# Chunked attention and two mixtures of experts: outputs of two attention tiles and scores of the next two in one run of small products

## Chip, cores and metric

The kernel runs on one core of a Trainium2 chip. The metric is the device time of one execution in microseconds (us). The core has TensorE (PE: matrix products; its weight loads are listed apart as PEld), VectorE (DVE), ScalarE (ACT), GpSimd (POOL) and SyncE (SP, which issues DMAs). Products are written to PSUM, which has eight banks of 512 fp32 columns on each of the 128 partitions.

## Reference

```python
def _attn_ref(q, k, v):                     # B, H, S, D = 8, 8, 576, 64
    q_c = q.reshape(B, H, nc, 64, D)        # chunks of 64 positions; k_c, v_c alike
    scores = scale * np.matmul(q_c, k_c.transpose(0, 1, 2, 4, 3))
    scores = scores - np.max(scores, axis=-1, keepdims=True)
    attn = np.exp(scores)
    attn = attn / (np.sum(attn, axis=-1, keepdims=True) + 1e-09)
    return np.matmul(attn, v_c).reshape(B, H, S, D)

def _moe_ref(x, w1, w2, w3, w_out):         # x 4608 x 512, w 512 x 768
    h = np.maximum(np.maximum(x @ w1, x @ w2), x @ w3)
    return h @ w_out

def _moe2_ref(x, w_gate, w_output_gate, w1, w2):   # 8 experts, 512 -> 1024 -> 512
    e_idx = np.argmax(x @ w_gate, axis=1)
    ...                                     # gate_w: softmax at e_idx; eom: sigmoid
    for e in range(E):
        mask = e_idx == e
        out[mask] = gate_w * eom[mask, e] * (np.maximum(x[mask] @ w1[e], 0.0) @ w2[e])
```

## The kernel before

The program has two parts, one after the other, and TensorE works through both.

**First part: attention and the first mixture.** The 4608 tokens are 36 tiles of 128, in nine blocks of four. A tile has two chunks of 64 positions and eight heads, so its scores are 16 products of 64x64 (line 440, `att_S`), and its outputs 16 more (line 520, `att_V`; line 518 for the first four tiles). Between the two lie the softmax (DVE maximum, ACT exponentials, DVE or POOL division) and four transposes of the probabilities into the PSUM bank `tr0` or `tr1` by the tile's parity (`att_P`, line 495), which ACT copies to `pTF` (line 501). Outputs go to SBUF in two parts, high (`xth`, ACT, line 532) and low (`xtl`, DVE). Scores and outputs share the two banks of one PSUM tile `a2`: scores in one half of each bank, outputs in the other (`quarters`). From tile 7 on `att_V(i)` issues the outputs of tile i and the scores of tile i+1 as one piece. The mixture's products (`moe_f`, 18 groups of 12 products of 128x512 for a block; `moe_y`, products of 256 or 272 columns) fill TensorE's time between; three products (lines 102 to 104) make one of higher precision.

The order of the first part isn't written by hand. Every operation is recorded with `add(...)`: engine, a duration, a due time (`prio`), and the keys that it reads and writes. `order()` then plays the program through with these durations and issues, on each engine, the ready operation with the earliest due time; the result is a fixed order for each engine. Waits between engines are set afterwards by the tile framework, from the tiles that the instructions read and write. In the first 30 us the planner also puts in small bf16 products that compute nothing (`warm`, line 291), written to whichever of `tr1`, `psg`, `tr0` is free.

**Second part: the routed experts.** 21 blocks of up to 256 tokens are run, each with its expert's weights (`step(b)`, and block 0 by lines of its own behind line 1247). A block with two tiles of tokens ("full") takes the first branch of `step`: the first layer (`l1_mm`), the transposes of the next block's tokens (`x_T`), the second layer of tile 0 (`l2(b, 0)`: 24 products of 128x512 into `ps_y[0]`), `y_act(b, 0)` (line 930: ACT reads `ps_y[0]`, scales it and writes `yo`), and `l2(b, 1)` into `ps_y[1]`. `ps_y` is another name for the two banks `tr0` and `tr1`. Other blocks take the second branch, with `l2(b, 0)` alone.

```python
    ps_y = ps_tr
...
            convs(b, 1)
            l2(b, 0)
            y_act(b, 0)
            l2(b, 1)
```

Of the kernel before, what the change touches and what calls it, by code (L numbers as in the profile page):

```python
# [10 lines left out]
F32 = mybir.dt.float32  # L11
# [10 lines left out]
def tile_chunk_attention_moe_moe(  # L22
# [16 lines left out]
    PE, ACT, DVE, POOL, SP = nc.tensor, nc.scalar, nc.vector, nc.gpsimd, nc.sync  # L39
# [7 lines left out]
    P = 128  # L47
    NTILE = NT // P
# [16 lines left out]
    tile_block = {}  # L65
# [10 lines left out]
    psp = ctx.enter_context(tc.tile_pool(name="psp", bufs=1, space=bass.MemoryType.PSUM))  # L76
# [16 lines left out]
    NAT, SUBD = 4, (0, 2)  # L93

    def f(ap):
        return ap.bitcast(F32)

    def sub(eng, o, a, b):
        eng.tensor_tensor(out=o, in0=a, in1=b, op=ALU.subtract)  # L99
# [72 lines left out]
    HP = H // 2  # L172
# [6 lines left out]
    v_buf = [part(n, i, 1).rearrange("p (h c d) -> p h c d", h=HP, c=2) for n, i in ((1, 2), (1, 3), (2, 3))]  # L179
    es = [part(2, i, 1).rearrange("p (h j) -> p h j", h=H) for i in range(3)]  # L180
    pTF = [part(3, i, 1).rearrange("p (a c i) -> p a c i", a=HP, c=2) for i in range(2)]
# [56 lines left out]
    rfv = gview(2 * TB, F32, "p (a t) -> p a t", t=TB)  # L238


    ps_tr = [psp.tile([P, 512], F32, name=f"tr{i}", tag=f"tr{i}") for i in range(2)]
    ps_a2 = psp.tile([P, 1024], F32, name="a2", tag="a2")
    ps_mm = [psp.tile([P, 512], F32, name=f"mm{i}", tag=f"mm{i}") for i in range(3)]
    ps_g = psp.tile([P, 512], F32, name="psg", tag="psg")
# [114 lines left out]
    def t_act(n):  # L359
        return 0.055 + n / 1200  # L360

    def t_dve(n, fast=False):
        return 0.067 + n / (1920 if fast else 960)
# [34 lines left out]
    def h64(h2):  # L398
        return slice(64 * h2, 64 * h2 + 64)
# [3 lines left out]
        i = a % NE2  # L403
        return es[i], [("e", i), ("mx", i), ("sm", i)], mxs[i], sms[i]

    def quarters(a, h=0):


        sp = lambda x, n: x.rearrange("p (b x) -> p b x", b=n)[:, :, h * HP * 64:(h + 1) * HP * 64].rearrange(
            "p b (a i) -> p b a i", a=HP)  # L410
        if a % 3 and a < NW:
            bk = [(ps_mm[0], ("mm", 0)), (ps_mm[1], ("mm", 1))] if a % 3 == 1 else [(ps_mm[2], ("mm", 2)), (ps_g, "psg")]
            return [(sp(x, 1), [kx], slice(i, i + 1)) for i, (x, kx) in enumerate(bk)]
        return [(sp(ps_a2, 2), ["a2"], slice(0, 2))]

    def add_sub(eng, n, prio, rd, wr, o, a, b):
# [5 lines left out]
    def att_Q(a, pr):  # L422
        for w in range(2):
            load(a, w, pr - LA)

    def att_S(a, pr, alone=True):


        e, (ek, mk, sk), mx, sm = e_of(a)

        t = qk_buf[a % 3]
        parts = quarters(a)
        bank = [ps[:, i] for ps, _, hs in parts for i in range(hs.stop - hs.start)]

        def mm():
            for hp in range(HP):
                for h2 in range(2):
                    for c in range(2):
                        x = t[h64(h2), :, hp, h64(c)]
                        PE.matmul(bank[h2 if a < NAT else h2 ^ c][h64(c), hp], x[:, 0], x[:, 1], start=True, stop=True)  # L440

        if not alone:
            yield mm
        else:
            add("PE", T_Q, pr + 1, [("qk", a % 3, 0), ("qk", a % 3, 1)], [x for _, kk, _ in parts for x in kk], mm)
        m2 = mx.rearrange("p (b a) -> p b a", b=2)
        for n, (ps, pk, hs) in enumerate(parts):
            add("DVE", t_dve(512 // len(parts)), pr + 1, pk, [(mk, n)],
                lambda ps=ps, hs=hs: DVE.tensor_reduce(out=m2[:, hs], in_=ps, axis=AX.X, op=ALU.max))
        ex = e.rearrange("p (a b) j -> p b a j", b=2)  # L450
        ek2, sk2 = [(ek, 0), (ek, 1)], [(sk, 0), (sk, 1)]
        if a in SUBD:
            for n, (ps, pk, hs) in enumerate(parts):
                add("DVE", t_dve(512 // len(parts)), pr + 1, pk + [(mk, n)], ek2 if len(parts) == 1 else [(ek, n)],
                    lambda ps=ps, hs=hs: DVE.tensor_tensor(
                        out=ex[:, hs], in0=ps, in1=m2[:, hs].unsqueeze(3).to_broadcast([P, hs.stop - hs.start, HP, 64]),
                        op=ALU.subtract))
            add("ACT", t_act(512), pr + 1, ek2, ek2, lambda: ACT.activation(out=e, in_=e, func=ACTF.Exp, scale=scale))
            add("DVE", t_dve(512), pr + 1, ek2, sk2, lambda: DVE.tensor_reduce(out=sm, in_=e, axis=AX.X, op=ALU.add))
        else:  # L460
            add("DVE", 0.08, pr + 1, [(mk, n) for n in range(len(parts))], [mk] + [(mk, n) for n in range(len(parts))],
                lambda: DVE.tensor_scalar(out=mx, in0=mx, scalar1=-scale, scalar2=None, op0=ALU.mult))  # L462
            for b in range(2):
                ps, pk, hs = parts[b % len(parts)]

                def fn(b=b):
                    for hp in range(HP):
                        ACT.activation(  # L468
                            out=ex[:, b, hp], in_=bank[b][:, hp], func=ACTF.Exp, scale=scale,
                            bias=mx[:, HP * b + hp:HP * b + hp + 1], accum_out=sm[:, 2 * hp + b:2 * hp + b + 1])  # L470

                add("ACT", 4 * 0.29, pr + 1, pk + [mk], [(ek, b), (sk, b)], fn)
        add("DVE", 0.08, pr + 1, sk2, sk2,
            lambda: DVE.tensor_scalar(out=sm, in0=sm, scalar1=1e-9, scalar2=None, op0=ALU.add))
        add("DVE", 0.12, pr + 1, sk2, sk2, lambda: DVE.reciprocal(out=sm, in_=sm))
        on = "DVE" if a < MULD else "POOL"
        add(on, t_dve(512) if on == "DVE" else 1.0, pr + 1, ek2 + sk2, ek2,
            lambda: (DVE if on == "DVE" else POOL).tensor_tensor(
                out=e, in0=e, in1=sm.unsqueeze(2).to_broadcast([P, H, 64]), op=ALU.mult))
        yield  # L480
# [19 lines left out]
        add("PE", 0.9 if a < NAT else 0.45, pr + 2, [(ek, 0), (ek, 1)], [("tr", a % 2)], fn)  # L500
        add("ACT", t_act(512), pr + 2, [("tr", a % 2)], [("pTF", a % 2)], lambda: ACT.copy(pTF[a % 2], pp))

    def att_V(a, pr, score=None):

        j, t_ = tile_block[a]
        dst = lambda hl: xt[j % 2][hl][:, :, t_ * P:(t_ + 1) * P]
        xk = lambda hl: [("xt", j % 2, t_, hl, h2) for h2 in range(2)]
        vv, x = v_buf[a % NV], pTF[a % 2]
        parts = quarters(a, 1 if score else 0)
        bank = [ps[:, i] for ps, _, cs in parts for i in range(cs.stop - cs.start)]  # L510
        with_it = next(score) if score else None

        def mm():
            for hp in range(HP):
                for s in range(2):
                    for c in range(2):
                        if a < NAT:
                            PE.matmul(bank[c][h64(s), hp], vv[h64(c), hp, s], x[h64(c), hp, s], start=True, stop=True)
                        else:
                            PE.matmul(bank[c][h64(s ^ c), hp], vv[h64(s), hp, c], x[h64(s), hp, c], start=True, stop=True)  # L520

            if with_it:
                with_it()

        qk = [("qk", (a + 1) % 3, w) for w in range(2)] if score else []
        add("PE", 2 * T_Q - 0.3 if score else T_Q, pr + 3, [("v", a % NV), ("pTF", a % 2)] + qk,
            [x for _, kk, _ in parts for x in kk], mm)
        o = lambda hl: dst(hl).rearrange("p a (b i) -> p b a i", b=2)
        for ps, pk, cs in parts:
            n = 256 * (cs.stop - cs.start)  # L530
            kx = lambda hl: [("xt", j % 2, t_, hl, i) for i in range(cs.start, 2)] if n == 256 else xk(hl)
            add("ACT", t_act(n), pr + 3, pk, kx(0), lambda ps=ps, cs=cs: ACT.copy(o(0)[:, cs], ps))
            add("DVE", t_dve(n), pr + 3, pk + kx(0), kx(1), lambda ps=ps, cs=cs: sub(DVE, o(1)[:, cs], ps, f(o(0)[:, cs])))


    def words(src):
# [559 lines left out]
    def attention(a, n):  # L1096

        def prio(i):
            j, t = tile_block[i]
            return -100 + PS * i if j == 0 else A1 + AS1 * t if j == 1 else v0(j - 1) + AO + AS * t  # L1100

        pr = [prio(i) for i in range(NTILE)]

        def score(i):
            att_Q(i, pr[i])
            next(att_S(i, pr[i]))


        before = {i: [i + 2] for i in (*range(NA - 2), NA, NA + 1)}
        after = {NA - 1: [NA, NA + 1]}  # L1110
        if a == 0:
            score(0)
            score(1)
        for i in range(a, a + n):
            att_P(i, pr[i])
            for x in before.get(i, ()):
                score(x)

            s_ = None
            if 2 * NA - 1 <= i < NTILE - 1:  # L1120
                att_Q(i + 1, pr[i + 1])
                s_ = att_S(i + 1, pr[i + 1], False)
            att_V(i, pr[i], s_)
            if s_:
                next(s_)
            for x in after.get(i, ()):
                score(x)

# [182 lines left out]
```

## Time and profile before

| | |
|---|---|
| time, median of 3 runs | 1166.98 us (1165.87 to 1168.24) |
| time of the profiled execution | 1168.08 us |
| its span, first to last instruction | 1166.4 us |
| mean granted TensorE clock | 0.995 of full speed |
| PE busy | 1147.5 us, 98% of the span |
| DVE, ACT, POOL busy | 426.7, 414.3, 194.4 us |

The span is one profiled execution; the remaining 1.7 us of its time lie around it. Products overlap in TensorE, so what one product costs is read from the distance between the starts of two, not from its own length.

### The profile page before, as it was taken

How to read it: one execution, taken by the hardware profiler on the slowest of the kernel's cores; microseconds unless marked ns; L12 is line 12 of the kernel's file. 1: busy time of each engine (PE TensorE's matmuls, PEld its weight loads, DVE VectorE, ACT ScalarE, POOL GpSimd, SP SyncE). 2: the span in 40 equal slices, each digit the busy share in tenths (PEclk: the TensorE clock that was granted, in tenths of full speed). 3: DMA queues.
4: the chain of work that ended last, by engine and by line, in shares of the span. 5: the costliest groups of instructions: out<-in, count | busy, mean ns of one | idle time of the engine just before them, and what ended most of it. 6: DMA issues, size and time to landing. Idle time of an engine off the chain costs nothing.

```text
span 1166.4 us, 22880 instructions
## 1 busy us (share of the span) xinstructions
PE 1147.5 (98%) x8963; PEld 1011.0 (87%) x8963; DVE 426.7 (37%) x1087; ACT 414.3 (36%) x1192; POOL 194.4 (17%) x243
## 2 busy tenths in 40 slices
PE   7999999999999999999999999999999999999997
PEld 6779889888898888988989889999898999899976
DVE  7996523223232242322323335112136511422163
ACT  5566333333333233332321332222236522422173
POOL 1000120211202112112111211221113121121122
PEclk9999999999999999999999999999999999999999
DMA  8743322112211122121221004321136611241151
GB/s 283 234 136 101 91 56 65 55 28 92 55 64 56 28 91 55 56 64 28 83 71 66 28 1 151 114 65 38 38 120 214 244 61 42 77 169 38 47 195 42
DMA packets 84335, 103.28 MB, mean 89 GB/s; under 512 B 40287, under 2 KB 49503, under 8 KB 84192
## 3 DMA queue, kind: packets, MB, share of 16 engines
q1 hardware_dynamic: 77152, 79.82, 21.4%
q0 software_dynamic: 7040, 21.60, 5.7%
q8 instruction: 85, 1.39, 0.5%
q14 instruction: 58, 0.48, 0.1%
HBM read 149.55 MB, written 20.52 MB: 146 GB/s over the span
## 4 chain that ended last, share of the span: by engine, by line
PE 91%; DVE 3%; DMA 2%; issue 1%; ACT 1%; POOL 0%; SPq 0%; POOLq 0%; ACTq 0%
PE mm L102 21%; PE mm L103 21%; PE mm L104 21%; PE tr L104 6%; PE tr L102 6%; PE tr L103 6%; DMA wst<-in_moe_w_dram 2%; PE a L520 2%; PE a L863 2%; PE psg L104 1%; PE psg L103 1%; PE psg L102 1%; PE a L440 1%; PE tr L495 1%; DVE wpc L99 1%
## 5 line engine op out<-in xcount | busy, mean ns | idle before, releaser
L102 PE MATMUL mm<-xth,wpc 128*128 128x512 f32 x576 | 229.4, 398 | 0.0
L104 PE MATMUL mm<-xth,wpc 128*128 128x512 f32 x576 | 225.0, 391 | 0.0
L103 PE MATMUL mm<-xtl,wpc 128*128 128x512 f32 x576 | 224.5, 390 | 0.0
L631 DVE TENSOR_TENSOR hs<-mm,hs 128x512 f32<-128x512 f32 x108 | 74.5, 690 | 221.6 <-PE mm L104 221.6
L104 PEld LDWEIGHTS mm<-xth,wpc 128*128 128x128 f32 x576 | 108.1, 188 | 23.2
L102 PEld LDWEIGHTS mm<-xth,wpc 128*128 128x128 f32 x576 | 108.1, 188 | 22.2
L103 PEld LDWEIGHTS mm<-xtl,wpc 128*128 128x128 f32 x576 | 108.3, 188 | 20.7
L102 PE MATMUL mm<-wo,ht 128*128 128x256 f32 (+1 forms) x432 | 125.4, 290 | 0.0
L104 PE MATMUL mm<-wo,ht 128*128 128x256 f32 (+1 forms) x432 | 122.8, 284 | 0.0
L103 PE MATMUL mm<-wo,ht 128*128 128x256 f32 (+1 forms) x432 | 122.5, 284 | 0.0
L102 PE MATMUL tr<-wpc,wo 128*128 128x512 f32 x304 | 120.2, 396 | 0.0
L104 PE MATMUL tr<-wpc,wo 128*128 128x512 f32 x304 | 118.5, 390 | 0.0
L103 PE MATMUL tr<-wpc,wo 128*128 128x512 f32 x304 | 118.3, 389 | 0.0
L891 DVE SCALAR_TENSOR_TENSOR wo<-mm,wo 128x512 fp32r<-128x512 f32 x52 | 35.5, 690 | 200.4 <-ACT wo L887 170.6
L99 POOL TENSOR_TENSOR ht<-hs,ht 128x512 fp32r<-128x512 f32 x48 | 61.7, 1286 | 183.8 <-ACT ht L633 183.8
L468 ACT ACTIVATE rg<-a,mx 128x64 f32<-128x64 f32 x264 | 79.1, 325 | 33.5 <-DVE mx L462 33.4
L102 PEld LDWEIGHTS mm<-wo,ht 128*128 128x128 f32 x432 | 81.3, 188 | 0.9
L103 PEld LDWEIGHTS mm<-wo,ht 128*128 128x128 f32 x432 | 81.5, 189 | 0.4
L104 PEld LDWEIGHTS mm<-wo,ht 128*128 128x128 f32 x432 | 81.2, 188 | 0.0
L99 DVE TENSOR_TENSOR wpc<-raw,wpc 128x512 fp32r<-128x512 f32 x112 | 70.0, 685 | 30.3 <-ACT wpc L845 30.3
L930 ACT ACTIVATE yo<-tr,xg 128x512 f32<-128x512 f32 x42 | 28.5, 688 | 136.9 <-PE tr L104 136.9
L933 POOL DMA_INDIRECT out_dram<-yo,S x30 | 31.9, 1062 | 241.4 <-ACT yo L930 166.7
(269 smaller groups left out, 2161.0 us busy)
## 6 DMA issues: line engine op xcount, KB each, us to landing
raw<-in_moe_w_dram SPq DMA_DIRECT2D x92, 1024.0 KB
x_scratch<-U SPq DMA_DIRECT2D x36, 258.0 KB
rg<-in_q_dram SPq DMA_DIRECT2D x36, 256.0 KB
rg<-in_k_dram SPq DMA_DIRECT2D x36, 256.0 KB
wst<-in_moe_w_dram SPq DMA_DIRECT2D x18, 512.0 KB
rg<-in_v_dram SPq DMA_DIRECT2D x128, 64.0 KB
U<-in_moe_w_out_dram SPq DMA_DIRECT2D x6, 512.0 KB
rg<-in_v_dram SPq DMA_DIRECT2D x4, 256.0 KB
```

Of the source, the lines that this page charges most:

```text
L99: eng.tensor_tensor(out=o, in0=a, in1=b, op=ALU.subtract)
L102: PE.matmul(o, ah, bh, start=first, stop=False)
L103: PE.matmul(o, ah, bl, start=False, stop=False)
L104: PE.matmul(o, al, bh, start=False, stop=last)
L440: PE.matmul(bank[h2 if a < NAT else h2 ^ c][h64(c), hp], x[:, 0], x[:, 1], start=True, stop=True)
L468: ACT.activation(out=ex[:, b, hp], in_=bank[b][:, hp], func=ACTF.Exp, scale=scale, bias=mx[:, HP * b + hp:HP * b + hp + 1], accum_out=sm[: ...
L520: PE.matmul(bank[c][h64(s ^ c), hp], vv[h64(s), hp, c], x[h64(s), hp, c], start=True, stop=True)
L631: add("DVE", t_dve(N), up, [pk, hk], [hk], lambda: DVE.tensor_tensor(out=h, in0=ps, in1=h, op=ALU.max))
L863: PE.transpose(ps_x[:, kk, t * P:(t + 1) * P], xg(b)[:, t, kk * P:(kk + 1) * P], ident)
L891: DVE.scalar_tensor_tensor(out=hT()[:, 1, fs], in0=l1_ps(c), scalar=0.0, in1=f(hT()[:, 0, fs]), op0=ALU.max, op1=ALU.subtract)
L930: ACT.activation(out=yo(b, t), in_=ps_y[t], func=ACTF.Copy, scale=xg(b)[:, t, DM:DM + 1])
L933: POOL.indirect_dma_start(out=out, out_offset=bass.IndirectOffsetOnAxis(ap=ic[b % 4]()[:, t, 1:2].bitcast(U32), axis=0), in_=yo(b, t), in_ ...
```

## The change

Three things are edited. The two banks `tr0` and `tr1` become the two halves of one PSUM tile `t2`. From tile 8 on, the outputs of two tiles (an even one and the odd one behind it) are issued in one piece with the scores of the next two tiles; tile 7's outputs go with the scores of tiles 8 and 9, and the outputs of tiles 34 and 35 stand alone. And these outputs are written to `t2` (the even tile in one half of both banks, the odd tile in the other), while `a2` holds the scores of two tiles.

```diff
-    ps_tr = [psp.tile([P, 512], F32, name=f"tr{i}", tag=f"tr{i}") for i in range(2)]
+    ps_t2 = psp.tile([P, 1024], F32, name="t2", tag="t2")
+    ps_tr = [ps_t2[:, i * 512:(i + 1) * 512] for i in range(2)]
...
-    def quarters(a, h=0):
+    def quarters(a, h=0, tr=False):
...
+        if tr:
+            return [(sp(ps_t2, 2), [("tr", 0), ("tr", 1)], slice(0, 2))]
         return [(sp(ps_a2, 2), ["a2"], slice(0, 2))]
...
     def att_S(a, pr, alone=True):
...
-        parts = quarters(a)
+        parts = quarters(a, 0 if alone else a % 2)
...
-    def att_V(a, pr, score=None):
...
+    def att_V(a, pr):
+        outputs([a], pr, False)
+
+    def outputs(tiles, pr, tr=True, scores=(), nexts=()):
+
+        parts, mms = {}, []
+        for a in tiles:
+            parts[a] = quarters(a, a % 2 if tr else 0, tr)
...
+            mms.append(mm)
+        mms += [next(x) for x in scores]
+        rd = [k for a in tiles for k in (("v", a % NV), ("pTF", a % 2))] + [("qk", a % 3, w) for a in nexts for w in range(2)]
+        wr = [x for a in tiles for _, kk, _ in parts[a] for x in kk] + (["a2"] if nexts else [])
+        add("PE", T_Q + 0.47 * (len(mms) - 1), pr + 3, rd, list(dict.fromkeys(wr)), lambda: [mm() for mm in mms])
+        for a in tiles:
...
+                add("ACT", t_act(n), pr + 3, pk, kx(0), lambda ps=ps, cs=cs, o=o: ACT.copy(o(0)[:, cs], ps))
+                add("DVE", t_dve(n), pr + 3, pk + kx(0), kx(1),
+                    lambda ps=ps, cs=cs, o=o: sub(DVE, o(1)[:, cs], ps, f(o(0)[:, cs])))
...
-            s_ = None
-            if 2 * NA - 1 <= i < NTILE - 1:
-                att_Q(i + 1, pr[i + 1])
-                s_ = att_S(i + 1, pr[i + 1], False)
-            att_V(i, pr[i], s_)
-            if s_:
-                next(s_)
+
+            if i < 2 * NA - 1:
+                att_V(i, pr[i])
+            elif i % 2:
+                nexts = [x for x in (i + 1, i + 2) if x < NTILE]
+                for x in nexts:
+                    att_Q(x, pr[x])
+                ss = [att_S(x, pr[x], False) for x in nexts]
+                outputs([i] if i < 2 * NA else [i - 1, i], pr[i], True, ss, nexts)
+                for x in ss:
+                    next(x)
```

How it moves instructions is seen in three places. First TensorE in the first part, a run of small products behind the transposes of a tile and twelve large products, before (line 520 outputs, line 440 scores, 16 of 64x64 for a tile):

```order
L104 MATMUL mm2_160<-xth0_133,wpc0_144 128x512
L520 MATMUL a2_157<-rg3_125,rg1_123 64x64 x16
L440 MATMUL a2_157<-rg1_123 64x64 x16
L102 MATMUL mm0_158<-xth0_133,wpc0_144 128x512
```

and of the change (line 523 outputs, line 442 scores):

```order
L104 MATMUL mm2_159<-xth0_133,wpc0_144 128x512
L523 MATMUL t2_155<-rg3_125,rg1_123 64x64 x32
L442 MATMUL a2_156<-rg1_123 64x64 x16
L442 MATMUL a2_156<-rg0_122 64x64 x16
L102 MATMUL mm0_157<-xth0_133,wpc0_144 128x512
```

The run has 64 products instead of 32. Before, TensorE's order has 28 runs of 32 and one of 16 from tile 7's outputs on; now it has 13 of 64, one of 48 and one of 32. A middle block of four tiles had four runs, three among products of 512 columns and one among the 256- and 272-column products of `moe_y`; now it has two, both among products of 512 columns. The transposes (line 495, now 497) still stand tile by tile.

Second, TensorE in the second part, where a full block goes from `l2(b, 0)` to `l2(b, 1)`, before (with the engines that an instruction waits for):

```order
L104 MATMUL tr0_155<-wpc3_147,wo_149 128x512 [waits DVE_49]
L102 MATMUL tr0_155<-wpc3_147,wo_149 128x512
L103 MATMUL tr0_155<-wpc3_147,wo_149 128x512
L104 MATMUL tr0_155<-wpc3_147,wo_149 128x512
L102 MATMUL tr1_156<-wpc2_146,wo_149 128x512
L103 MATMUL tr1_156<-wpc2_146,wo_149 128x512
```

and of the change:

```order
L104 MATMUL t2_155<-wpc3_147,wo_149 128x512 [waits DVE_49]
L102 MATMUL t2_155<-wpc3_147,wo_149 128x512
L103 MATMUL t2_155<-wpc3_147,wo_149 128x512
L104 MATMUL t2_155<-wpc3_147,wo_149 128x512
L102 MATMUL t2_155<-wpc2_146,wo_149 128x512 [waits Activation_49]
L103 MATMUL t2_155<-wpc2_146,wo_149 128x512
```

The products are the same; the first one of `l2(b, 1)` (weights `wpc2` again) now carries a wait for ScalarE. The only ScalarE instruction between the two groups in the program is `y_act(b, 0)`. The same stands in every full block and in block 0; the rest of the second part is unchanged on every engine.

Third, TensorE in the first 30 us, the `warm` products between the transposes of tile 2 (line 494) and its outputs (line 521), of the change:

```order
L494 MATMUL t2_155<-ident_72,rg2_124 64x64 x15
L292 LDWEIGHTS ones_b_77
L292 MATMUL t2_155<-ones_b_77 128x128
...
L292 MATMUL t2_155<-ones_b_77 128x128 [waits Activation_49]
...
L521 MATMUL mm2_159<-rg3_125,rg2_124 64x64 [waits DMAHW4_49]
```

Before, none of these eleven waits for ScalarE; now the fifth does. One of the ten behind tile 0's transposes (the third) has the same new wait.

## Rows read from the trace of the kernel before

**Rows 1.** Windows: busy us (instructions) of each engine, granted clock, DMA share, GB/s

```profile
90.00:613.00 523.00, 523.00 (x4591) 452.30 (x4590) 167.07 (x536) 181.95 (x714) 83.06 (x100) 1.00 0.21 63
728.00:897.00 169.00, 169.00 (x1092) 154.67 (x1091) 44.56 (x68) 48.54 (x84) 33.41 (x39) 1.00 0.29 97
```

**Rows 2.** Timeline (start, us, ...) of PE around a run of two tiles' products

```profile
219.68 0.40 PE L104 MATMUL mm<-xth,wpc 128*128 128x512 f32 x1
...
221.10 0.50 PE L102 MATMUL mm<-xth,wpc 128*128 128x512 f32 x1
221.43 0.39 PE L103 MATMUL mm<-xtl,wpc 128*128 128x512 f32 x1
```

**Rows 3.** Timeline of PE around the run of one tile's outputs

```profile
606.64 0.40 PE L104 MATMUL mm<-xth,wpc 128*128 128x512 f32 x1
606.97 0.69 PE L520 MATMUL a<-rg,rg 64*64 64x64 f32 x32
607.59 0.50 PE L102 MATMUL mm<-xth,wpc 128*128 128x512 f32 x1
```

**Rows 4.** Timeline of PE around a run among 256-column products

```profile
187.90 0.28 PE L103 MATMUL mm<-wo,ht 128*128 128x256 f32 x1
188.02 0.28 PE L104 MATMUL mm<-wo,ht 128*128 128x256 f32 x1
...
189.31 0.39 PE L102 MATMUL mm<-wo,ht 128*128 128x256 f32 x1
189.54 0.28 PE L103 MATMUL mm<-wo,ht 128*128 128x256 f32 x1
```

**Rows 5.** Timeline from the end of l2(b, 0) on, a full block

```profile
820.44 0.39 PE L104 MATMUL tr<-wpc,wo 128*128 128x512 f32 x1
...
820.66 0.39 PE L102 MATMUL tr<-wpc,wo 128*128 128x512 f32 x1
...
820.86 0.69 ACT L930 ACTIVATE yo<-tr,xg 128x512 f32<-128x512 f32 x1 [3.54 <-PE tr L104]
...
825.88 0.39 PE L104 MATMUL tr<-wpc,wo 128*128 128x512 f32 x1
```

**Rows 6.** Timeline where PE waits for ACT; brackets: idle before, releaser

```profile
1008.06 0.60 ACT L906 ACTIVATE U<-mm 128x512 f32<-128x512 f32 x1 [2.12 <-PE mm L104]
...
1008.71 0.66 PE L910 MATMUL psg<-ident,U 128*128 128x128 f32 x4 [0.30 <-ACT U L906]
```

**Rows 7.** Groups by form: xcount, busy us, mean ns, idle before

```profile
L102 PE MATMUL tr<-wpc,wo 128*128 128x512 f32 x304 | 120.2, 396 | 0.0
...
L102 PEld LDWEIGHTS tr<-wpc,wo 128*128 128x128 f32 x304 | 57.1, 188 | 11.1
...
L930 ACT ACTIVATE yo<-tr,xg 128x512 f32<-128x512 f32 x42 | 28.5, 688 | 136.9 <-PE tr L104 136.9
```

**Rows 8.** Timeline of block 0, between its two second layers

```profile
726.77 0.69 ACT L930 ACTIVATE yo<-tr,xg 128x512 f32<-128x512 f32 x1 [4.87 <-PE tr L104]
...
727.36 0.48 PE L102 MATMUL tr<-wpc,wo 128*128 128x512 f32 x1
```

**Rows 9.** Timeline of the start, tile 2

```profile
20.86 0.79 PE L291 MATMUL tr<-ones_b 128*128 128x128 bf16 x11
21.02 0.58 ACT L501 COPY rg<-tr 128x512 f32<-128x512 f32 x1 [0.91 <-PE tr L492]
...
21.66 0.27 PE L518 MATMUL mm<-rg,rg 64*64 64x64 f32 x1
```

**Rows 10.** Windows, as rows 1; the granted clock follows the five engines

```profile
87.00:90.00 3.00, 3.00 (x9) 2.32 (x9) 3.00 (x8) 2.51 (x5) 0.00 (x0) 0.50 0.78 220
1127.00:1131.00 4.00, 2.93 (x22) 2.32 (x21) 3.32 (x6) 3.46 (x8) 0.00 (x0) 1.00 1.04 371
```

**Rows 11.** Timeline of PE: two waits of about 1 us

```profile
84.93 0.69 PE L440 MATMUL a<-rg 64*64 64x64 f32 x32 [0.99 <-DVE xtl L99]
...
1128.61 0.66 PE L910 MATMUL mm<-ident,U 128*128 128x128 f32 x4 [1.07 <-ACT U L906]
```

More of the change, by code (lines that the diff above doesn't have):

```diff
@@ L501, in att_P @@
         add("ACT", t_act(512), pr + 2, [("tr", a % 2)], [("pTF", a % 2)], lambda: ACT.copy(pTF[a % 2], pp))
-    def att_V(a, pr, score=None):
[L505 to L533, printed above, removed]
@@ new lines, in att_V, with mm @@
+    def att_V(a, pr):
[4 more added lines that the diff above has]
+            parts[a] = quarters(a, a % 2 if tr else 0, tr)
+            bank = [ps[:, i] for ps, _, cs in parts[a] for i in range(cs.stop - cs.start)]
+            def mm(a=a, bank=bank):
+                vv, x = v_buf[a % NV], pTF[a % 2]
+                for hp in range(HP):
+                    for s in range(2):
+                        for c in range(2):
+                            if a < NAT:
+                                PE.matmul(bank[c][h64(s), hp], vv[h64(c), hp, s], x[h64(c), hp, s], start=True, stop=True)
+                            else:
+                                PE.matmul(bank[c][h64(s ^ c), hp], vv[h64(s), hp, c], x[h64(s), hp, c], start=True, stop=True)
+            mms.append(mm)
[4 more added lines that the diff above has]
+        for a in tiles:
+            j, t_ = tile_block[a]
+            dst = lambda hl, j=j, t_=t_: xt[j % 2][hl][:, :, t_ * P:(t_ + 1) * P]
+            xk = lambda hl, j=j, t_=t_: [("xt", j % 2, t_, hl, h2) for h2 in range(2)]
+            o = lambda hl, dst=dst: dst(hl).rearrange("p a (b i) -> p b a i", b=2)
+            for ps, pk, cs in parts[a]:
+                n = 256 * (cs.stop - cs.start)
+                kx = lambda hl: [("xt", j % 2, t_, hl, i) for i in range(cs.start, 2)] if n == 256 else xk(hl)
+                add("ACT", t_act(n), pr + 3, pk, kx(0), lambda ps=ps, cs=cs, o=o: ACT.copy(o(0)[:, cs], ps))
+                add("DVE", t_dve(n), pr + 3, pk + kx(0), kx(1),
+                    lambda ps=ps, cs=cs, o=o: sub(DVE, o(1)[:, cs], ps, f(o(0)[:, cs])))
```

## The prediction

> **What bounds the kernel now.** I read first the windows, one for the middle of each part [rows 1]. In both PE is busy for the whole window at the full clock (523.00 of 523.00 us, 169.00 of 169.00), while DVE, ACT and POOL have 167, 182 and 83 of the 523 us, and DMA a share of 0.21 and 0.29. So from 90 us on the kernel is one row of products behind each other: whatever lengthens or shortens PE's row by a microsecond moves the end by as much, and work on the other engines counts only where PE is made to wait for it. The next views are therefore timelines of PE, at the two places where the change touches its row.
>
> Products overlap, so I price by the distance between two starts. Between products of 512 columns it is 0.227 us: 23 distances from 820.66 to 825.88 [rows 5]. Between products of 256 columns it is 0.12 (187.90 to 188.02) [rows 4].
>
> **Part one: fewer, longer runs of small products.** A run holding two tiles' products (outputs of one, scores of another) stands between the 512-column products at 219.68 and 221.10, 1.42 us instead of 0.227, and the distance after the first large product is 0.33 instead of 0.227 [rows 2]. That is 1.19 + 0.10 = 1.30 us for the run. The one run of a single tile, the outputs of the last tile, takes 606.64 to 607.59, 0.95 us [rows 3], 0.47 less. So the products of one tile cost 0.47 us, those of two 0.94, and 1.30 - 0.94 = 0.36 us is the price of entering and leaving small products, paid once a run. Among 256-column products it is alike: 188.02 to 189.31 is 1.29 instead of 0.12, then 0.23 instead of 0.12 [rows 4]: 1.28 - 0.94 = 0.34.
>
> The change keeps every product and takes 29 runs to 15. In a middle block one of the two runs that go is of the first kind and one of the second, so 7 x 0.36 + 7 x 0.34 = 4.9 us are saved. From below I bound it by the two pieces that I can see directly, the late entry (606.64 to 606.97 is 0.33 instead of 0.227) and the late product after the run, 0.10 each: 14 x 0.20 = 2.8. From above, by what two decimals allow, 14 x 0.40 = 5.6. I take 4.9, since the two run lengths give the whole price and not pieces.
>
> What I cost at nothing here. Behind a run ACT and DVE now have two tiles' outputs to copy out and two tiles' scores to turn into probabilities, in a burst; no product of the mixture needs the scores before the next transposes, over 60 products or 13 us later, and both engines have two thirds of the window free [rows 1]. The query, key and value loads keep their due times, and queues with a share of 0.21 don't notice two tiles' loads together. The common tile `t2` has a side effect here too: the transposes of the odd tile must now wait until ACT has copied those of the even one. About 60 large products lie between the two, 13.6 us, against a copy of 0.58 [rows 9]. If that cover were gone, it would be 0.58 + 0.05 in each of 14 pairs, 8.8 us.
>
> **Part two: a wait between the two second layers.** This is the larger term. `l2(b, 0)` and `l2(b, 1)` wrote to two tiles; they now write to two halves of one. The order of the change shows what comes of it: the first product of `l2(b, 1)` waits for ScalarE, and the only ScalarE instruction between is `y_act(b, 0)`, which can't begin before the last product of `l2(b, 0)` has ended. Before, PE went through: the last product started at 820.44, the next at 820.66, while ACT took 820.86 to 821.55 beside it [rows 5]. Now the next product follows ACT. How soon, I read where PE does wait for ACT: ACT ends at 1008.06 + 0.60 = 1008.66, PE starts at 1008.71, 0.05 later [rows 6]. So the product starts at 820.86 + 0.69 + 0.05 = 821.60, which is 0.94 us late. PE then starts anew; the trace has no 512-column product behind a bare wait. Nothing lost is the lower end, and a whole weight load, 0.188 [rows 7], the upper. I take 0.10, as large products lose behind a run of small ones [rows 2], that being the nearest case of a large product whose predecessor had left the engine. That makes 1.04 us for each full block, between 0.94 and 1.13.
>
> How many full blocks are run: `yo` is written 42 times, twice a block, so 21 blocks. `l2` has 8 products of line 102, and 304 of them are 38 layers [rows 7]. Block 0 has two of these; with F full blocks among the other 20, 2F + (20 - F) = 36, F = 16. Thus 16 x 1.04 = 16.6 us, between 15.0 and 18.1. Nothing takes it back: behind the waiting product stand on PE the 24 products of `l2(b, 1)` and the whole next block, and in the last full block the final copy and its scatter. The few waits of PE on ACT in the other blocks come from PE's own products a moment earlier, so they move along.
>
> In block 0 the transposes of the next block stand between the two layers and hide most of the wait: ACT ends at 726.77 + 0.69 = 727.46, so PE may start at 727.51, where it started at 727.36 [rows 8]: 0.15 us, between 0 and 0.3.
>
> **The start.** The same coupling makes `warm` products wait for ACT's copy of a transpose. For tile 2 eleven of them run 20.86 to 21.65 while ACT copies, and the outputs start at 21.66 [rows 9]. Now seven of the eleven come behind the copy, some 0.5 us before the outputs may start; for tile 0 eight of ten. Part of this is lost on conversions and loads that run beside it. I take 0.3 us, between 0 and 1.0 (both delays in full).
>
> **The sum**, against the profiled execution: -4.9 + 16.6 + 0.15 + 0.3 = +12.2 us, 1168.08 to 1180.3. That execution lay 1.1 us above the median of 1166.98, so the forecast is 1179.2 us. With all bounds at one end the difference is 15.0 - 5.6 = +9.4, at the other 18.1 - 2.8 + 0.3 + 1.0 = +16.6: 1176.4 to 1183.6.
>
> **Rivals.** *The wait costs nothing* (the other side). The place is the same product; the other terms stay, -4.9 + 0.3, and the time is 1162.4 us. It decides from where the wait is worth less than 4.9 / 16 = 0.31 us a block. For it speaks that the two layers touch different banks, so nothing in the data needs a wait. Against it: the wait stands in the order, and ACT's instruction alone is 0.69 us and begins only after the last product [rows 5]. 4 in 100. The Trainium skill, "PSUM — Partial Sum Buffer", section "PSUM bank collisions raise a hardware error", says that TensorE may write one bank while another engine reads a different one, and asks for a guard by bank; by that rule alone the wait would not be there and the time would be this rival's 1162.4. The trace before agrees with the rule, since ACT read one bank beside products into the other from 820.86 on; but a wait that the program carries is paid whether the banks need it or not.
>
> *The long runs make PE wait in the first part.* If the cover of the odd tile's transposes, or of the evictions behind a run, fails in each pair, 8.8 us come on top: 1188.0. Against it speak the idle shares [rows 1]; for it, that the planner orders by its own durations, not by measured ones. 6 in 100.
>
> *The clock falls at the new waits.* The profile has one place where something like it happened: PE waited 0.99 us at 84.93 amid light products [rows 11], and the stretch from 87 to 90 was granted 0.50, the 1.2 GHz level [rows 10]. Behind a wait of 1.07 us at 1128.61 [rows 11], amid large products as in the new case, the clock stayed at 1.00, 2.4 GHz [rows 10]. Half speed for 3 us loses 1.5; in each of 16 blocks that is 24 us, 1203. 4 in 100. Once or twice is within the range.
>
> **How the numbers follow.** The forecast has 86 in 100, its rivals 4, 6 and 4. The range is the forecast's own bounds, 1176 to 1184, rounded outward; it leaves out the three rivals and a little of the forecast. 0.2% is 2.3 us, about what a measurement of this kernel can tell. Faster by more than that: 0.04, the first rival. Within it: 0.01, were the waits to eat just what the runs save. Slower: 0.95.
>
> **What would show it.** In the profile of the changed kernel, PE should have an idle time of about 0.77 us, released by ACT's `yo`, in front of the first product of `l2(b, 1)`, 16 times, with 1.16 us between the two starts where 0.22 stood. A middle block's two runs should each show 2.36 us between the large products around them (0.95 + 3 x 0.47), and the first part from 90 to 613 us should end 4 to 5 us earlier. PE's waits of 90 to 613 us should stay near none, and the granted clock of the second part at 1.00. The prediction is wrong if that idle time is absent or under 0.3 us, if PE waits at the transposes, or if stretches of the second part show 0.50.

## The result, and the profile after

| | before | after |
|---|---|---|
| time, median of 5 runs | 1167.05 us | 1179.33 us |
| lowest to highest | 1165.87 to 1168.24 us | 1179.00 to 1180.49 us |
| span of the profiled execution | 1166.4 us | 1177.3 us |
| mean granted clock | 0.995 | 0.998 |

The changed kernel takes 1.0112 times as long (95% interval 1.0100 to 1.0124), 12.3 us more by the medians. The forecast was 1179.2 us.

The windows of the first part's middle and of seven full blocks in the second part, columns as in [rows 1]:

```profile
90.00:613.00 523.00, 523.00 (x4612) 455.38 (x4612) 173.24 (x537) 181.15 (x715) 85.50 (x101) 1.00 0.21 64
728.00:897.00 169.00, 163.42 (x1047) 146.87 (x1046) 43.17 (x66) 46.35 (x80) 31.92 (x38) 1.00 0.26 85
```

In the first part PE is still busy throughout. In the second it is idle 5.58 of 169 us where it had no idle time, at the same clock of 1.00. The list of PE's waits from 720 us on says for what:

```profile
PE t L102 <- ACT yo L937: 12.4, 16, 0.8
PE mm L917 <- ACT U L913: 1.1, 1, 1.1
PE psg L917 <- ACT U L913: 0.9, 3, 0.3
PE mm L102 <- ACT yo L937: 0.8, 1, 0.8
```

The first line is the forecast wait, 16 times 0.78 us; the second and third were there before [rows 6, 11], the third one time less; the last is new and wasn't foreseen. One of the sixteen in the timelines of PE and ACT, to be held against [rows 5]:

```profile
816.68 0.39 PE L104 MATMUL t<-wpc,wo 128*128 128x512 f32 x1
...
817.84 0.50 PE L102 MATMUL t<-wpc,wo 128*128 128x512 f32 x1 [0.78 <-ACT yo L937]
818.18 0.40 PE L103 MATMUL t<-wpc,wo 128*128 128x512 f32 x1
818.42 0.40 PE L104 MATMUL t<-wpc,wo 128*128 128x512 f32 x1
...
817.10 0.69 ACT L937 ACTIVATE yo<-t,xg 128x512 f32<-128x512 f32 x1 [3.54 <-PE t L104]
```

ACT ends at 817.79 and PE starts at 817.84: 1.16 us from start to start, 0.94 us later than the 0.227 between products puts it, and the next distance is 0.34 instead of 0.227. And the run of four tiles' products in the first part, to be held against [rows 2]:

```profile
230.94 0.40 PE L104 MATMUL mm<-xth,wpc 128*128 128x512 f32 x1
231.27 1.16 PE L523 MATMUL t<-rg,rg 64*64 64x64 f32 x64
232.25 1.11 PE L442 MATMUL a<-rg 64*64 64x64 f32 x64
233.29 0.50 PE L102 MATMUL mm<-xth,wpc 128*128 128x512 f32 x1
233.63 0.40 PE L103 MATMUL mm<-xtl,wpc 128*128 128x512 f32 x1
```

It stands 2.35 us between the large products (forecast 2.36), then 0.34.

To see where time goes I cut every profiled execution at the same products: the 217th product of `moe_f` (the first one of the second block of tiles, at about 120 us), its last one, and the program's last product. In us:

| execution | start to 217th | 217th to last of `moe_f` | to PE's last product | to the end |
|---|---|---|---|---|
| before | 121.98 | 567.67 | 469.35 | 7.38 |
| after | 118.99 | 563.36 | 488.55 | 6.41 |
| difference | -2.99 | -4.31 | +19.19 | -0.97 |

The third column holds 13 of the 14 runs that went. It also takes in the outputs of tile 8, 0.47 us of products that stood ahead of it before: (4.31 + 0.47) / 13 is 0.37 a run. The second column has the other run and those outputs, 0.8, and 2.2 us that the forecast didn't have. The fourth column is 16 blocks of 1.11 us, 17.8, block 0 with 0.2, and about 1.1 at the unforeseen wait.

### The profile page after: what moved, and what is told of

Read it like the earlier page. It is cut to its first block, busy times and chain, and to the rows that moved or that the text cites. A ratio compares the mean times of both kernels' runs of the same rounds, so it can differ in the third digit from the quotient of the medians.

```text
span 1177.3 us, 22871 instructions
## 1 busy us (share of the span) xinstructions
PE 1147.1 (97%) x8963; PEld 1007.8 (86%) x8963; DVE 432.6 (37%) x1087; ACT 413.1 (35%) x1192; POOL 195.7 (17%) x243
## 4 chain that ended last, share of the span: by engine, by line
PE 88%; DVE 4%; issue 3%; DMA 2%; ACT 1%; POOL 1%; POOLq 0%; SPq 0%; ACTq 0%; DVEq 0%
PE mm L102 20%; PE mm L104 20%; PE mm L103 20%; PE t L102 6%; PE t L104 5%; PE t L103 5%; PE a L870 1%; PE t L523 1%; PE psg L104 1%; PE psg L103 1%; PE psg L102 1%; PE a L442 1%; PE t L497 1%; ACT yo L937 1%; DMA wst<-in_moe_w_dram 1%
## 5 line engine op out<-in xcount | busy, mean ns | idle before, releaser
L102 PE MATMUL t<-wpc,wo 128*128 128x512 f32 x304 | 122.4, 403 | 12.4 <-ACT yo L937 12.4
L103 PE MATMUL t<-wpc,wo 128*128 128x512 f32 x304 | 118.9, 391 | 0.0
L104 PE MATMUL t<-wpc,wo 128*128 128x512 f32 x304 | 118.6, 390 | 0.0
L102 PEld LDWEIGHTS t<-wpc,wo 128*128 128x128 f32 x304 | 57.1, 188 | 30.3 <-ACT yo L937 19.2
L937 ACT ACTIVATE yo<-t,xg 128x512 f32<-128x512 f32 x42 | 28.4, 687 | 155.0 <-PE t L104 155.0
```

The costliest lines, as they stand in the source:

```text
L102: PE.matmul(o, ah, bh, start=first, stop=False)
L103: PE.matmul(o, ah, bl, start=False, stop=False)
L104: PE.matmul(o, al, bh, start=False, stop=last)
L937: ACT.activation(out=yo(b, t), in_=ps_y[t], func=ACTF.Copy, scale=xg(b)[:, t, DM:DM + 1])
```

## Experiments

Theory: the loss is the wait that the common tile puts between the two second layers, and the gain is the price of entering and leaving small products, once a run. Rivals: the long runs lose the time; the gain comes from the new banks.

**Two tiles again.** The changed kernel with the two banks as two PSUM tiles; each output is copied out bank by bank.

```diff
-    ps_t2 = psp.tile([P, 1024], F32, name="t2", tag="t2")
-    ps_tr = [ps_t2[:, i * 512:(i + 1) * 512] for i in range(2)]
+    ps_tr = [psp.tile([P, 512], F32, name=f"tr{i}", tag=f"tr{i}") for i in range(2)]
...
-            return [(sp(ps_t2, 2), [("tr", 0), ("tr", 1)], slice(0, 2))]
+            return [(sp(ps_tr[i], 1), [("tr", i)], slice(i, i + 1)) for i in range(2)]
```

> The changed kernel's runs of 64 products, but tr0 and tr1 two PSUM tiles again (outputs copied out bank by bank). My theory (the time is lost in the wait of l2(b,1) for y_act(b,0), 16 times 1.11 us, and won in the first part by fewer runs): the wait is gone, 1179.3 - 17.8 - 0.2 = 1161.3 us, 1160 to 1163, no PE idle time in front of l2(b,1), next large product 0.22 us on. Rival (the long runs themselves or the banks of the outputs lose the time): 1177 to 1180, as the changed kernel.

Measured: 1162.89 us, 0.9976 of before (0.9966 to 0.9985). The 16 waits are gone and the runs' gain stays (563.36 us in the third column). The long runs lose nothing.

**The common tile alone.** The kernel before with that edit the other way round.

> The kernel before with one edit alone: tr0 and tr1 become halves of one PSUM tile; runs of small products as before. My theory: the whole loss comes back without the gain, 1167.05 + 17.8 + 0.2 = 1185 us, 1183.5 to 1186.5, with 0.78 us of PE idle time 16 times. If also the 2.2 us that the changed kernel won ahead of 100 us come from the common tile (its warm products in other places), 1183. Rival (the tile costs nothing): 1167.

Measured: 1186.48 us, 1.0180 of before (1.0163 to 1.0196), with the same first line in its list of waits:

```profile
PE t L102 <- ACT yo L931: 12.4, 16, 0.8
```

Its third column is 567.68, as before, its fourth 488.43, as after. So the edit of the tile carries the whole loss and the edit of the runs the whole gain. It is 1.5 us above the 1185 expected; the fourth column again holds about 1.1 us of the unforeseen wait.

**Another bank for the second layer.** The changed kernel with one line changed, which sends `l2(b, 1)` to the bank `psg`; its first part is untouched.

```diff
-    ps_y = ps_tr
+    ps_y = [ps_tr[0], ps_g]
```

> The changed kernel with one edit: in the second part l2(b,1) writes to the bank psg instead of the second half of t2; the first part is the changed kernel's to the last instruction. My theory: the wait is gone, 1161.3 us, 1160 to 1163; and if the 2.2 us won ahead of 100 us come from the common tile, this kernel keeps them and the one with two tiles does not (2 us between the two). Rival (the loss lies in the first part): 1177 to 1180.

Measured: 1162.78 us, 0.9979 of before (0.9966 to 0.9992). PE goes through again beside ACT's reading:

```profile
834.88 0.39 PE L104 MATMUL t<-wpc,wo 128*128 128x512 f32 x1
835.11 0.39 PE L102 MATMUL psg<-wpc,wo 128*128 128x512 f32 x1
...
835.30 0.69 ACT L937 ACTIVATE yo<-t,xg 128x512 f32<-128x512 f32 x1 [3.56 <-PE t L104]
```

Both kernels lie in the range expected, but 1.6 and 1.5 us above the 1161.3 that was worked out. The list of waits of this one has a new line for that, which is taken up below with the jump:

```profile
PE mm L102 <- ACT wpc L852: 1.6, 1, 1.6
```

**Work over the wait.** The common tile stays, and the next block's transposes are put into the wait.

```diff
-            x_T(b + 1)
             convs(b, 1)
             l2(b, 0)
             y_act(b, 0)
+            x_T(b + 1)
             l2(b, 1)
```

> The changed kernel, common tile and all, but in full blocks the next block's 8 transposes stand between y_act(b,0) and l2(b,1) instead of in front of l2(b,0), as in block 0. My theory: the wait stays in the program but work lies over it, about 0.15 us a block is left as in block 0 (+0.20 there): 1179.3 - 16 x 0.95 = 1164 us, 1162 to 1167. Rival (a wait between the two layers is paid whatever stands in it, by the stop of the queue): within 2 us of 1179.

Measured: 1169.89 us, 1.0039 of before (1.0025 to 1.0053). The mechanism held, a full block takes 23.51 us instead of 24.41 (23.30 before), but the sum didn't: 4.9 us are lost at the first products behind a block of one tile, 1.6 us in each of three places like this one:

```profile
904.92 0.39 PE L104 MATMUL t<-wpc,wo 128*128 128x512 f32 x1
906.02 0.38 PE L102 MATMUL mm<-wo,wpc 128*128 128x256 f32 x1 [0.71 <-ACT wpc L852]
906.80 0.38 PE L103 MATMUL mm<-wo,wpc 128*128 128x256 f32 x1 [0.39 <-DVE wpc L99]
```

These products need the transposed tokens, and they wait for conversions of weights. A wait here is for a count of an engine's finished instructions, one number for both branches that lead to it. My edit put the copies of the tokens behind the conversions in the full branch; in the other branch, where the conversions stand behind the copies, the same count is reached only by the conversions. That is how I read the program; the next run tests it.

**The same with the order mended.**

```diff
-            convs(b, 1)
             l2(b, 0)
             y_act(b, 0)
             x_T(b + 1)
+            convs(b, 1)
             l2(b, 1)
```

> The changed kernel with the 8 transposes of the next block between the two layers, as in the run with the cover, but the conversions of the second weight slice left behind the transposes' copies, as in the changed kernel. That run had 1.1 us of PE idle time at the start of three blocks behind a block of one tile, where a first product waited for a count of ScalarE that the other branch reaches with its conversions. My theory (that wait comes from the order of copies and conversions): the three waits go, 1169.9 - 3 x 1.3 = 1166 us, 1165 to 1167.5. Rival (it comes from the transposes' place): 1169.5 to 1171.

Measured: 1163.99 us, 0.9983 of before (0.9973 to 0.9994); the three waits are gone. It is 2 us better than expected. The three waits had cost 1.6 us each and not the 1.3 that I took, which is 1.0 of it; the rest I did not take apart. ACT runs 837.27 to 837.96 here, and the second layer starts 0.05 later:

```profile
836.84 0.39 PE L104 MATMUL t<-wpc,wo 128*128 128x512 f32 x1
837.07 1.03 PE L870 MATMUL a<-ident,xg 128*128 128x128 f32 x8
838.01 0.50 PE L102 MATMUL t<-wpc,wo 128*128 128x512 f32 x1
```

So 0.21 us a block are left of 1.11.

**The price of a run, by cutting.** The kernel with the other bank, its long runs cut in two:

```diff
-                outputs([i] if i < 2 * NA else [i - 1, i], pr[i], True, ss, nexts)
+                outputs([i] if i < 2 * NA else [i - 1, i], pr[i])
+                if nexts:
+                    ms = [next(x) for x in ss]
+                    add("PE", T_Q + 0.47 * (len(ms) - 1), pr[i] + 6, [("qk", a % 3, w) for a in nexts for w in range(2)],
+                        ["a2"], lambda ms=ms: [mm() for mm in ms])
```

> The kernel with l2(b,1) in psg, but each long run of small products cut in two: the outputs of two tiles, and some 3 us of large products later the scores of two. Same products, same banks, 14 runs more from tile 8 on. My theory (0.36 us for entering and leaving, paid once a run): 14 x 0.36 = +5.0, 1162.8 to 1167.8 us, 1166.5 to 1169. Rival (the first part's gain came from the new banks or from fewer copies and waits, not from the number of runs): 1162 to 1164.

and in four, one tile's outputs or scores each:

```diff
-                outputs([i] if i < 2 * NA else [i - 1, i], pr[i], True, ss, nexts)
+                for n, a in enumerate([i] if i < 2 * NA else [i - 1, i]):
+                    outputs([a], pr[i] + 3 * n)
+                for n, (a, x) in enumerate(zip(nexts, ss)):
+                    mm = next(x)
+                    add("PE", T_Q, pr[i] + 9 + 3 * n, [("qk", a % 3, w) for w in range(2)], ["a2"], mm)
```

> The same kernel with each long run cut in four, one tile's outputs or scores each: 3 x 13 + 2 = some 41 runs more than the kernel with l2(b,1) in psg. My theory: 41 x 0.36 = +14.8, 1177.6 us, 1174 to 1182 (upper end if PE also waits for copies out of the common tiles between two of them). Rival: 1162 to 1164.

Measured: 1168.48 us (1.0018 of before, 1.0008 to 1.0028) and 1175.96 us (1.0083, 1.0068 to 1.0098), 5.7 and 13.2 us above the uncut kernel. The timeline of the first shows both halves at the price of [rows 2]:

```profile
232.93 0.40 PE L104 MATMUL mm<-xth,wpc 128*128 128x512 f32 x1
233.26 1.16 PE L523 MATMUL t<-rg,rg 64*64 64x64 f32 x64
234.35 0.50 PE L102 MATMUL mm<-xth,wpc 128*128 128x512 f32 x1
...
235.61 0.39 PE L104 MATMUL mm<-xth,wpc 128*128 128x512 f32 x1
235.93 1.16 PE L442 MATMUL a<-rg 64*64 64x64 f32 x64
237.02 0.50 PE L102 MATMUL mm<-xth,wpc 128*128 128x512 f32 x1
```

1.42 and 1.41 us. The first has 13 runs more (in one place the planner set two pieces side by side), all behind the 217th product, and its third column grows from 563.37 to 568.33: 0.38 each. The second has 41 more, 40 of them in the third column, which is 15.4 us longer (578.76): 0.39 each. It is the number of runs that costs, in the same banks. The time of the second rises by less than that, mostly because its jump (below) costs nothing (fourth column 469.46 against 471.31).

**The same kernels once more.** Two things were left: the start, and the wait at 897 us.

> The kernel before once more, unchanged, for a second profiled execution. Theory (the stretches at the 1.2 GHz level ahead of 100 us, and the time that TensorE's queue takes for the jump to the branch of the one-tile blocks, differ from execution to execution): other stretches and another jump time than in the first profile, the first part's end moved by up to 3 us, and 0 us between the two from 100 us to the end of the first part. Rival (they belong to the program): the same stretches, the same jump time.

> The changed kernel once more, unchanged. The same question: by the first theory the time ahead of 100 us moves by up to 3 us and the idle time of 0.81 us at the first block of one tile may be absent; by the rival both come again. In either case 16 idle times of 0.78 us in front of l2(b,1).

> The kernel with l2(b,1) in psg once more, unchanged. By the first theory the idle time of 1.65 us at its first block of one tile (queue busy 4.67 us with the jump) may be absent; by the rival it comes again with 4.6 to 4.7 us.

| execution | time | start to 217th | 217th to last of `moe_f` | to PE's last product | to the end |
|---|---|---|---|---|---|
| before | 1168.08 | 121.98 | 567.67 | 469.35 | 7.38 |
| before, again | 1165.32 | 118.75 | 567.68 | 469.41 | 7.70 |
| after | 1179.00 | 118.99 | 563.36 | 488.55 | 6.41 |
| after, again | 1180.91 | 120.86 | 563.36 | 488.29 | 6.61 |
| other bank | 1161.38 | 117.41 | 563.37 | 471.31 | 7.60 |
| other bank, again | 1163.08 | 118.96 | 563.37 | 471.41 | 7.64 |

The third column repeats within 0.01 us, the fourth within 0.3. The start does not repeat: 1.6 to 3.2 us lie between two executions of one kernel. In [rows 10] the kernel before was at the 1.2 GHz level from 87 to 90 us; in its second execution the window shows 2.4 GHz, and so it is from 29 to 32 us (0.50 in the first, 1.00 in the second):

```profile
87.00:90.00 3.00, 3.00 (x18) 2.48 (x16) 3.00 (x7) 1.86 (x4) 0.00 (x0) 1.00 0.70 230
```

So my first theory held for the start and fell for the wait at 897: that one belongs to the program. What it is shows in the branch instructions of PE's queue (count, then lowest, median and highest duration in ns), here around that place before, after, and with the other bank:

```profile
L1207 PEldq COMPARE_BRANCH  x2: 190/1121/2052, 892.0 to 892.9; - x2
```

```profile
L1218 PEldq COMPARE_BRANCH  x2: 291/2069/3847, 892.6 to 893.7; - x2
```

```profile
L1218 PEldq COMPARE_BRANCH  x2: 286/2478/4671, 883.1 to 884.1; - x2
```

It is the jump to the branch for blocks of one tile, at the first of them: 2.05, 3.85 and 4.67 us, and in the second executions 1.98, 3.69 and 4.69. (The shorter of the two entries is the jump at the end of the full block just before.) PE's queue comes to it 2.9 to 3.1 us before the next product is due. What is longer leaves PE idle: with the other bank the jump begins at 884.11 and ends at 888.78, the products would go on at 887.14, and they do at 888.95. With two tiles the first jump took 4.65 us and the second 3.80, which leaves PE idle a second time, by 0.8 us. The releaser that the list of waits names there (`yo` in one kernel, `wpc` in another) only happened to end near by.

**The load away from the jump.** With the other bank, loads of the next weights fill the DMA engines (40 slices of 0.3 us, the jump begins in the middle):

```profile
DMA  0000000546999999999999999999620100000020
```

```diff
             x_T(b + 1)
-            convs(b, 1)
             l2(b, 0)
             y_act(b, 0)
+            convs(b, 1)
             l2(b, 1)
```

> The kernel with l2(b,1) in psg, and in full blocks the conversions of the second weight slice behind y_act(b,0) instead of in front of l2(b,0), so that the load of the next weights (about 400 GB/s for 5.4 us around the jump to the first block of one tile) starts some 5 us later. Theory (the jump takes 4.7 us there because the instruction fetch shares the DMA engines with this load): the jump takes 2.0 to 2.5 us, the idle time of 1.65 us behind it goes, 1162.8 - 1.9 = 1160.9 us, 1159.5 to 1162. Rival (the jump's time has nothing to do with the load): 4.6 to 4.7 us and 1162.8 again, 1162 to 1164.

Measured: 1160.81 us, 0.9953 of before (0.9939 to 0.9967): the fastest of all. The DMA engines are quiet from the jump on, for 2.4 us, and the jump takes 2.51 us, below what is hidden:

```profile
DMA  0000000575999999991200000000999679999999
```

```profile
L1218 PEldq COMPARE_BRANCH  x1: 2507/2507/2507, 885.5 to 885.5; - x1
```

Its fourth column is 469.39, that of before. But the load isn't the whole of it: before had the same load at its jump and took 2.05 us, and so did the kernel with four runs, 2.09 us.

## Why the prediction was right

**The wait (+16.6).** The mechanism was right in each piece: 0.94 us late, 16 blocks, ACT's end 0.05 ahead of PE's start, and nothing takes it back. The restart was mis-sized: 0.10 taken, 0.17 measured (1.11 - 0.94), of which 0.11 is the first distance (0.34 instead of 0.227) and the rest the few behind it. The term is 17.8, within its bounds. The Trainium skill's rule ("PSUM — Partial Sum Buffer", section "PSUM bank collisions raise a hardware error") was no ground for the rival that the wait costs nothing; with two tiles or another bank the trace agrees with it, ACT reading beside products into the other bank, and the wait was there because the program's tile spans both.

**The runs (-4.9).** 13 x 0.37 behind the 217th product, and one more ahead of it: -5.1. Cutting gave 0.38 and 0.39 a run.

**Block 0 (+0.15).** 0.20.

**The start (+0.3).** The first two profiles show -2.2 in its place, after the run and the outputs of tile 8 are taken off; the repeats show that the start scatters by as much. For the common tile itself I have three executions with two tiles and ten with one: the 101st product of `moe_f` starts at 57.9 us in the mean of the first (57.3 to 58.9) and at 58.6 of the second (56.9 to 59.8). A delay of some 0.7 us is possible and not shown.

**Not in the sum.** The jump, +1.1, a step that the forecast had no term for: before, PE's queue was through the jump 1.0 us ahead of need (895.00 for the product at 896.01), and nothing of it shows in PE's row. And the end behind the last product, -1.0, which lies between 6.4 and 7.8 us in thirteen executions and which I didn't follow up. That the time agrees within 0.1 us is in part luck. The measured terms, 17.8 - 5.1 + 0.2 + 1.1 - 1.0, make +13.0 and not +12.2. The medians show 12.3, but the start scatters by more than these differ: the first profiled executions of the two kernels lie 10.9 us apart, the second ones 15.6, and later executions of the kernel before have medians of 1165.9 and 1166.0 us (23 each), some 1.1 below the five here.

**The rivals.** The wait was paid in full; PE waits nowhere from 90 to 690 us, so the long runs cost nothing; and the clock stayed at 1.00 behind all sixteen waits.

## What to carry to other kernels

Two buffers joined into one tile are one buffer to whoever sets the waits: look for every other use of the tile under another name, and price the wait there by what the reader of the first half takes, its latency and the restart. Where small products stand between large ones, the number of visits costs, not only their length. And a gain is kept by mending the step that lost: another bank for one layer, one line, turned +12.3 us into -3.2, and starting the next load of weights later, off the jump, made it -5.4.

## What the runs showed of the hardware

PE's queue has 36 compare-and-branch entries for `tc.If(full[b] > 0)` in each execution. The 16 that go on to the code behind took 65 to 89 ns, and the 16 jumps at the end of a full branch, over the branch for one tile, 169 to 325 ns. The four jumps over the full branch, to the branch for one tile, were of another kind: over all thirteen executions the first two took 2.0 to 4.7 us, the third 0.34 to 2.1 us and the fourth 0.34 to 0.35 us. The first one is the same within 0.2 us in two executions of a kernel and differs between kernels; the third of the changed kernel took 2.02 us in one execution and 1.44 in the other. The Trainium skill ("Advanced Engine Details and Errata", section "Control Flow Timing") gives about 108 ns for a compare-and-branch; here those that go on lie below it and every jump above it.

A jump is free as long as the queue runs further ahead of its engine than the jump takes, for the first one 2.4 to 3.1 us here. What sets its length is open. All seven first jumps above 3 us had a weight load of about 400 GB/s beside them, but so had those of 1.98, 2.05 and 2.09 us; the three with little on the DMA engines in their first 2 us took 2.29 to 2.51.
